# One late run of a causal convolution, moved from TensorE to VectorE and GpSimd

## The chip, the cores and the metric

The kernel runs on one core of one Trainium2 chip. The metric is the device time of one execution in microseconds (us), as the median of several runs; lower is better. A profile of one execution stands beside it, with the span from its first to its last instruction. The engines are called by the names of the profile: PE (TensorE, matmuls; PEld are its weight loads), DVE (VectorE), ACT (ScalarE), POOL (GpSimd) and SP (SyncE, which here only issues DMAs).

## The reference

Block-causal attention feeds a gated unit whose gate is a causal convolution in time. Inputs are q, k and v (8 batches, 8 heads, 576 positions, 64 features each), w_val and w_out (512 x 512) and conv_w (5 taps x 512 features):

```
mask   = block_i >= block_j                  # blocks of 64 positions
attn   = softmax(where(mask, q k^T / 8, -1e9))
x      = (attn v), heads side by side        # (8, 576, 512)
xp     = x with 4 zero rows in front of each batch
gate_pre[:, s, c] = sum over k < 5 of conv_w[k, c] * xp[:, s + k, c]
gate   = 1 / (1 + exp(-gate_pre))
out    = (gate * (x w_val)) w_out            # float32, (8, 576, 512)
```

The convolution is by feature: output feature c reads feature c alone, at five positions.

## The kernel before

**The order of the work.** A schedule written out in the string PLAN sets everything. Each word is one step, `name/arguments/engine/PSUM banks`, and the words are played in order: on each engine the instructions stand in the order of their words. "V/9.1/P/5" is step V for run 9 and quarter 1, on PE, into bank 5. The eight PSUM banks are handed out by hand, so a step that writes a bank waits for the step that read it last.

**Attention.** The work goes by p = 0 to 31, four pairs of heads for each of the eight batches (b = p // 4). `lq`, `lk`, `lv` load a block of 512 positions (v in two halves); `lt`, `lvt` load the last 64 positions of a batch. `cq`, `ct`, `cv`, `cvt` convert them to fp16 (mostly on POOL). `T`, `TT` transpose q and k on PE and `Te`, `TTe` copy them out of PSUM. `S` makes scores on PE, in three parts for each p, and `E` takes their exponential on ACT into the tile pt; `SL`, `EL` do so for the last block. `mka`, `mkb` write zeros over masked corners of pt (POOL). `A` and, once for a batch, `AT` multiply by v. `N`, `NT` divide by the sums (DVE). `X`, `XT` transpose the result and `Xe`, `XTe` copy it to xt, which holds features on partitions and positions along the free axis: four groups g of 128 features, and a ring of four batches of 4 + 576 columns, 2320 in all. Head pair p of batch b writes group g = p mod 4.

**The gated unit.** It does not follow batches but runs of RUN = 464 columns of the ring, five to a turn of the ring, n = 0 to 9. Run 7 covers ring columns 928 to 1392: the end of batch 5 and the first part of batch 6, so it needs `Xe` of p = 24 to 27. `C` computes the convolution of a run on PE: for each of five taps, 16 products with a diagonal 32 x 32 matrix of tap weights (tile DG, lines 585 to 595), 80 small matmuls into four banks. In doing so it moves the features: output partition 32 g + i of bank row x holds feature 128 g + 32 x + i, and `cwv` puts the columns of w_val in the same order, so that gate and value meet. `CS` takes tanh of half of it on ACT, two banks at a time, into the tile th (three buffers, run n in buffer n mod 3); `V` makes x w_val for a quarter of the features and a run; `Ve` computes (th + 1) times V into gv (DVE, line 614); the factor 0.5 is in w_out. `O u.t` multiplies 128 positions of gv by w_out (u is a pair of batches, t = 0 to 8; the last tile is split in two halves, `OL`), `Oe` copies the result to one of six osb tiles, `Od` stores it. Run 7 is read by O 2.7, O 2.8, O 3.0 and O 3.1.

**Weights of the taps.** `lcv` loads conv_w, `ccv` (line 362) makes it fp16, `CW` (line 551) turns it so that features lie on partitions, `CWe` copies it out and makes DG. `w0` are matmuls on zeros whose result nobody reads.

The shared helpers give one line to many steps in a profile: L137 are all matmuls, L141 all transposes on PE, L232 the copies by DVE and POOL, L230 those by ACT. L442 is E, L599 is CS, L614 is Ve.

The profiled program ends its PE order with: C 7, V 7.1, V 7.2, A 30, V 7.3, V 7.0, X 30, AT 7, C 8, V 8.0, XT 7, V 8.2, V 8.3, V 9.0, V 8.1, O 3.0, C 9, V 9.1, V 9.2, V 9.3, O 2.8, O 2.7, OL 1, OL 0, O 3.2, O 3.1, O 3.5, O 3.3, O 3.6, O 3.7, O 3.4.

Of the kernel before, what the change touches and what calls it, by code (L numbers as in the profile page):

```python
# [12 lines left out]
lk/0/S pdve//V ppool//G w0/1.128.0/P/3 lcv//S lq/0/S cq0/0/V ccv//G lk/1/S lq/1/A cq/1/V lt/0.0/S  # L13
lq/3/S lt/0.1/S lk/4/S lq/4/S ct/0/G lk/3/S CW//P/4 CWe//V lk/2/S lq/2/S cq/2/G lv/1.0/S lt/1.0/S
lv/0.0/S cq0/1/A pact//A T0/1/P/0+1 T0e/1/A lt/1.1/S T0/0/P/6+7 T0e/0/A S/0.1/P/5+6 T/1/P/0+1 Te/1/V
E/0.1/A lv/0.1/S lv/3.0/S lk/5/S lv/1.1/S lq/5/S S/0.0/P/5+6 E/0.0/A mka/0/G lt/2.0/S lt/2.1/S
lv/2.1/S lk/6/S TT/0/P/2+3 TTe/0/V SL/0/P/0+1 EL/0/A S/1.0/P/3+4 lv/3.1/S lq/6/S S/0.2/P/6+7
w0/1.64.1/P/5 E/1.0/A cq/4/V cq/3/V lvt/0/S E/0.2/A lv/2.0/S T/4/P/0+1 lq/8/S lk/8/S lq/7/S
S/1.1/P/2+3 E/1.1/A lk/7/S T/3/P/4+5 S/1.2/P/6+7 E/1.2/A Te/4/V S/4.0/P/0+1 lv/4.1/S T/2/P/2+3
E/4.0/A Te/3/V S/3.1/P/4+5 E/3.1/A mkb/0/G S/3.0/P/6+7 cv/0/G A/0/P/0+1 E/3.0/A S/4.1/P/4+5 Te/2/V  # L20
S/3.2/P/2+3 N/0/V mka/1/G cv/1/V ct/1/G cq/5/G TT/1/P/6+7 TTe/1/V w0/1.64.0/P/0 S/2.2/P/0+1 ct/2/G
E/4.1/A mkb/1/G mka/4/G E/3.2/A X/0/P/4+5 cv/3/G Xe/0/V E/2.2/A cq/6/G mkb/3/G mkb/2/G cvt/0/G
cv/2/G lv/7.0/S lv/5.0/S lv/4.0/S lwv/1/S S/2.1/P/2+3 E/2.1/A lwv/0/S lwo/0/S lwo/1/S T/5/P/4+5
Te/5/V lk/9/S lq/9/S lv/6.0/S lv/5.1/S cq/8/G lv/6.1/S lq/10/S lk/10/S mka/3/G cq/7/G lk/12/S
lq/12/S S/4.2/P/6+7 E/4.2/A mkb/4/G w0/1.64.0/P/0 S/2.0/P/0+1 E/2.0/A SL/1/P/2+3 EL/1/A A/1/P/4+5
N/1/V TT/2/P/6+7 TTe/2/V S/5.0/P/0+1 S/5.2/P/2+3 T/6/P/4+5 Te/6/V lq/13/S X/1/P/6+7 Xe/1/V E/5.0/A
lv/7.1/S lvt/1/S E/5.2/A mkb/5/G AT/0/P/0 NT/0/V lk/11/S lk/13/S lq/11/S S/6.1/P/4+5 S/6.0/P/6+7
SL/2/P/2+3 E/6.0/A EL/2/A T/8/P/0+1 Te/8/V A/3/P/6+7 N/3/V S/5.1/P/2+3 E/6.1/A T/7/P/0+1 Te/7/V
S/8.2/P/4+5 mka/2/G A/2/P/6+7 S/7.1/P/0+1 N/2/V E/5.1/A cwv/1/G cwv/0/G mka/5/G mka/6/G cwo/0/G
X/3/P/2+3 Xe/3/V E/8.2/A X/2/P/6+7 S/6.2/P/4+5 Xe/2/V E/7.1/A S/8.0/P/2+3 E/6.2/A cq/9/G mkb/8/G  # L30
E/8.0/A cv/5/G mkb/6/G cv/4/V C/0/P/0+1+6+7 A/4/P/4+5 XT/0/P/2 V/0.0/P/3 CS/0.1/A N/4/V X/4/P/4+5
CS/0.0/A Xe/4/A Ve/0.0/V S/7.0/P/0+1 E/7.0/A cwo/1/V XTe/0/V V/0.3/P/7 mka/7/G Ve/0.3/V V/0.2/P/3
Ve/0.2/V cv/6/G W//P/0+1+4+5 We/1/V S/7.2/P/6+7 V/0.1/P/2 We/0/A T/9/P/0+1 Te/9/V E/7.2/A
S/8.1/P/4+5 E/8.1/A A/5/P/6+7 S/9.0/P/0+1 A/6/P/4+5 Ve/0.1/V O/0.1/P/2 N/5/V E/9.0/A N/6/V X/5/P/0+1
Xe/5/A cq/10/G T/10/P/6+7 Te/10/V cq/12/G S/9.1/P/4+5 E/9.1/A O/0.2/P/3 Oe/0.2/V T/12/P/0+1 Te/12/V
S/10.0/P/6+7 mkb/7/G cv/7/G E/10.0/A cvt/1/G S/10.1/P/4+5 E/10.1/A O/0.0/P/3 X/6/P/6+7 Xe/6/A
Oe/0.0/A mka/8/G Oe/0.1/A lt/3.0/S lt/3.1/S A/7/P/0+1 AT/1/P/4 lv/8.0/S lt/4.0/S lt/4.1/S
S/12.0/P/6+7 mka/9/G lv/8.1/S N/7/V X/7/P/0+1 NT/1/V cq/11/G Xe/7/V lv/10.1/S E/12.0/A XT/1/P/5
XTe/1/V lv/10.0/S S/9.2/P/2+3 T/11/P/0+1 Te/11/V C/1/P/4+5+6+7 E/9.2/A cq/13/G T/13/P/2+3 V/1.1/P/0
CS/1.0/A lv/9.1/S Te/13/V lv/9.0/S lvt/2/S lv/11.1/S CS/1.1/A S/11.0/P/4+5 S/11.2/P/2+3 ct/3/G  # L40
TT/3/P/6+7 mkb/9/G TTe/3/V Ve/1.1/V cv/8/G V/1.3/P/1 Ve/1.3/V E/11.0/A lv/11.0/S lk/15/S
S/13.2/P/6+7 lq/15/S E/11.2/A S/10.2/P/4+5 mka/10/G lk/16/S V/1.0/P/0 Ve/1.0/V E/13.2/A A/8/P/2+3
N/8/V S/11.1/P/6+7 ct/4/G TT/4/P/0+1 TTe/4/V cv/10/G lq/16/S E/10.2/A lk/14/S lq/14/S V/1.2/P/5
Ve/1.2/V mkb/10/G mkb/11/G A/10/P/2+3 N/10/V mkb/13/G SL/3/P/0+1 E/11.1/A S/13.0/P/6+7 EL/3/A cv/9/G
E/13.0/A cvt/2/G A/9/P/4+5 X/8/P/0+1 Xe/8/A cv/11/G AT/2/P/2 S/12.1/P/6+7 E/12.1/A X/10/P/0+1 N/9/V
mka/11/G A/11/P/4+5 Xe/10/A O/0.3/P/3 NT/2/V XT/2/P/2 XTe/2/A lq/17/S SL/4/P/0+1 EL/4/A cq/15/G
T/15/P/6+7 N/11/V lk/17/S lv/13.1/S Oe/0.3/V S/13.1/P/4+5 Te/15/V O/0.4/P/2 S/12.2/P/0+1 lv/13.0/S
Od/0.0/S X/11/P/6+7 Oe/0.4/V lk/18/S lq/18/S E/13.1/A X/9/P/4+5 w0/1.64.1/P/3 w0/1.64.1/P/3
# [12 lines left out]
Xe/15/A Oe/0.8/V T/20/P/2+3 Te/20/A Xe/12/V lv/19.1/S lq/22/S lt/6.0/S lv/17.0/S X/14/P/4+5
S/19.1/P/0+1 E/19.1/A Xe/14/V X/13/P/6+7 A/16/P/4+5 lv/17.1/S lk/22/S Xe/13/V C/3/P/2+3+6+7 CS/3.0/A
N/16/V X/16/P/4+5 Xe/16/V lv/19.0/S lk/23/S Od/0.6/S O/0.7/P/0 cq/21/G lq/24/S Od/0.5/S T/21/P/2+3
Te/21/V lv/20.1/S lv/20.0/S CS/3.1/A lk/24/S Oe/0.7/V ct/6/G lq/23/S S/18.2/P/4+5 E/18.2/A mkb/18/G
cq/22/G V/3.2/P/1 Ve/3.2/V S/20.0/P/6+7 E/20.0/A C/4/P/2+3+4+5 CS/4.0/A V/3.3/P/0 Ve/3.3/V CS/4.1/A
V/3.1/P/7 Ve/3.1/V S/21.1/P/2+3 E/21.1/A mkb/17/G S/19.2/P/0+1 S/19.0/P/4+5 cv/18/G cvt/4/G cv/19/G
mka/17/G cv/17/G lt/7.1/S E/19.2/A mkb/19/G V/3.0/P/6 Ve/3.0/V V/4.3/P/3 lv/21.0/S lvt/5/S
TT/6/P/0+1 TTe/6/V E/19.0/A mka/19/G lq/25/S Od/0.7/S lv/21.1/S lk/25/S lt/7.0/S lk/26/S
S/20.2/P/6+7 E/20.2/A O/1.1/P/2 Ve/4.3/V S/20.1/P/0+1 E/20.1/A cq/24/G S/18.0/P/4+5 T/22/P/6+7
Te/22/V lq/26/S Oe/1.1/A O/1.2/P/3 A/17/P/0+1 E/18.0/A mka/18/G S/22.0/P/6+7 E/22.0/A AT/4/P/2  # L70
N/17/V X/17/P/4+5 S/21.0/P/0+1 E/21.0/A Xe/17/A A/19/P/6+7 Oe/1.2/V lv/23.1/S lv/23.0/S Od/1.1/S
lk/27/S O/1.3/P/3 NT/4/V lq/27/S XT/4/P/2 cq/23/G N/19/V lv/24.0/S lk/29/S S/21.2/P/0+1 T/24/P/6+7
# [40 lines left out]
def kernel(  # L113
# [44 lines left out]
    def one(b):  # L158
        return PS[0:128, b]
# [562 lines left out]
```

## Time and profile before

| | us |
|---|---|
| median of 3 runs | 187.36 |
| lowest, highest | 186.05, 188.68 |
| the profiled execution: its own time | 188.06 |
| its span, first to last instruction | 186.3 |
| PE, ACT, DVE, POOL busy | 164.2, 137.0, 125.1, 82.7 |
| last matmul ends, last copy out ends | 182.3, 182.9 |

The profiled execution's time is 1.76 us more than its span. A row of a timeline reads: start, duration, engine, line, operation, written tile <- read tiles, partitions x elements and type, xcount; in brackets the idle time of the engine before it and what ended it. Neighbouring instructions of one kind are merged into one row. A row by stretch reads: the stretch, its length, then busy time (and instructions) of PE, PEld, DVE, ACT and POOL, then the granted PE clock, the DMA share and GB/s. Of the chain by time, each row is a start, a length and what the chain went through.

### The profile page before, as it was taken

What the parts mean: (1) busy time and instruction counts of PE and PEld (TensorE: products, weight loads), DVE (VectorE), ACT (ScalarE), POOL (GpSimd) and SP (SyncE); (2) the same over time, 40 slices, a digit from 0 to 9 for tenths busy, and PEclk for the clock granted to TensorE, in tenths of its full rate; (3) what the DMA queues carried; (4) which work ended last, traced back from release to release, by engine and by line L of the source; (5) the groups of instructions that cost most, each with busy time, mean ns of one, the idle gap of its engine ahead of it and who ended that gap; (6) DMA issues with size and microseconds to landing.
All of it is one profiled execution on the core that took longest, in us unless ns stands there. A gap on an engine that the chain in (4) does not pass through costs nothing.

```text
span 186.3 us, 8262 instructions
## 1 busy us (share of the span) xinstructions
PE 164.2 (88%) x3534; PEld 101.4 (54%) x3534; DVE 125.1 (67%) x223; ACT 137.0 (74%) x164; POOL 82.7 (44%) x198
## 2 busy tenths in 40 slices
PE   1587638889999996999999999999999999999991
PEld 0364417754565774467645564656665575565540
DVE  5676636749977886777854677799787587533731
ACT  4489963698699885999969998897999842453431
POOL 6206449265682754556407455757590360000000
PEclk9999975699999999999999999999999999999999
DMA  6897896998966899769968888999998110351175
GB/s 184 261 286 180 223 262 172 291 328 243 267 165 157 224 308 300 191 165 327 273 157 272 239 245 260 298 286 282 222 276 231 69 60 0 141 204 57 69 281 217
DMA packets 66493, 40.38 MB, mean 217 GB/s; under 512 B 40213, under 2 KB 60949, under 8 KB 66458
## 3 DMA queue, kind: packets, MB, share of 16 engines
q1 hardware_dynamic: 66186, 39.61, 74.2%
q8 instruction: 27, 0.44, 1.0%
q10 hardware_dynamic: 272, 0.26, 0.4%
q14 instruction: 8, 0.07, 0.1%
HBM read 30.42 MB, written 9.44 MB: 214 GB/s over the span
## 4 chain that ended last, share of the span: by engine, by line
PE 74%; DMA 8%; DVE 5%; ACT 4%; SPq 4%; issue 3%; POOL 1%; DVEq 0%; ACTq 0%; POOLq 0%
PE PS L137 66%; PE PS L141 8%; DMA qks<-in_q_dram 3%; DMA qks<-in_k_dram 3%; ACT pt L442 3%; DMA vs<-in_v_dram 2%; DVE qkT L232 2%; SPq L244 2%; SPq L267 1%; DVE x L492 1%; ACT qkT L230 1%; POOL qk L232 1%; DVE rc L491 0%; DVE kt L232 0%; POOL v L232 0%
## 5 line engine op out<-in xcount | busy, mean ns | idle before, releaser
L442 ACT ACTIVATE pt<-PS 128x1024 f16<-128x1024 f32 x96 | 94.0, 1029 | 16.7 <-PE PS L137 15.1
L232 DVE COPY qkT<-PS 128x1024 f16<-128x1024 f16 x27 | 33.0, 1224 | 14.6 <-PE PS L141 13.7
L232 POOL CAST qk<-qks 128x1024 f16<-128x1024 f32 x28 | 29.1, 1042 | 25.3 <-DMA qks<-in_q_dram 14.8
L137 PE MATMUL PS<-qkT 64*128 64x384 f16 (+3 forms) x256 | 34.4, 319 | 2.9 <-ACT pt L442 1.6
L137 PE MATMUL PS<-xt,w_val 128*128 128x464 f16 x160 | 36.4, 360 | 0.0
L137 PE MATMUL PS<-w_out,gv 128*128 128x512 f16 (+2 forms) x164 | 35.5, 376 | 0.0
L137 PE MATMUL PS<-v,pt 128*128 128x65 f16 (+1 forms) x896 | 32.5, 198 | 2.4 <-POOL v L232 1.4
L137 PEld LDWEIGHTS <-pt 128*128 128x128 f16 (+1 forms) x960 | 29.5, 105 | 8.5 <-issue 4.5
L614 DVE SCALAR_TENSOR_TENSOR gv<-th,PS 128x464 f16<-128x464 f32 x40 | 24.6, 633 | 13.1 <-PE PS L137 7.8
L137 PEld LDWEIGHTS <-qkT 64*128 64x128 f16 x512 | 17.9, 97 | 16.6 <-issue 12.5
L599 ACT ACTIVATE th<-PS 128x928 f32<-128x928 f32 x20 | 17.9, 945 | 7.2 <-PE PS L137 7.0
L492 DVE TENSOR_TENSOR x<-PS,rc 128x512 f16<-128x512 f32 x32 | 22.1, 691 | 1.1
L232 POOL CAST v<-vs 128x512 f16<-128x512 f32 x30 | 18.5, 619 | 7.0 <-DMA vs<-in_v_dram 4.6
L137 PEld LDWEIGHTS <-w_val 128*128 128x128 f16 x160 | 13.5, 97 | 13.0 <-issue 2.4
L137 PEld LDWEIGHTS <-gv 128*128 128x128 f16 (+1 forms) x164 | 12.9, 100 | 12.9 <-issue 1.5
L141 PE MATMUL PS<-ident,qk 64*128 64x64 f16 x512 | 15.6, 202 | 3.3 <-POOL qk L232 3.0
L232 DVE COPY osb<-PS 128x512 f32<-128x512 f32 x20 | 13.7, 687 | 5.8 <-PE PS L137 5.8
L141 PEld LDWEIGHTS <-qk 64*128 64x128 f16 x512 | 12.4, 102 | 8.0 <-POOL qk L232 3.9
L464 POOL MEMSET pt<- 64x256 f16 x32 | 9.8, 306 | 13.3 <-ACT pt L442 12.2
L230 ACT COPY osb<-PS 128x512 f32<-128x512 f32 x15 | 8.7, 591 | 8.6 <-PE PS L137 8.4
L491 DVE RECIPROCAL rc<-PS 128x8 f32<-128x8 f32 x32 | 6.6, 206 | 12.2 <-PE PS L137 6.8
L137 PE MATMUL PS<-xt,DG 32*32 32x464 f16 x800 | 13.1, 358 | 0.4 <-ACT pt L442 0.3
(60 smaller groups left out, 136.4 us busy)
## 6 DMA issues: line engine op xcount, KB each, us to landing
out_dram<-osb SPq DMA_DIRECT2D x35, 256.0 KB, 3.9
qks<-in_k_dram SPq DMA_DIRECT2D x32, 256.0 KB, 4.8
vs<-in_v_dram SPq DMA_DIRECT2D x64, 128.0 KB, 4.4
qks<-in_q_dram SPq DMA_DIRECT2D x31, 256.0 KB, 5.2
tls<-in_q_dram SPq DMA_DIRECT2D x16, 64.0 KB, 3.5
tls<-in_k_dram SPq DMA_DIRECT2D x16, 64.0 KB, 3.6
vts<-in_v_dram SPq DMA_DIRECT2D x8, 128.0 KB, 5.2
gv<-in_moe_w_val_dram SPq DMA_DIRECT2D x2, 512.0 KB, 6.0
```

Source lines behind the costliest of these rows:

```text
L137: made.append(nc.tensor.matmul(out=out, lhsT=lhsT, rhs=rhs, start=start, stop=stop, skip_group_check=True))
L141: made.append(nc.tensor.transpose(out=out, in_=in_, identity=identity))
L230: i = nc.scalar.copy(out=out, in_=in_)
L232: i = (nc.vector if eng == "V" else nc.gpsimd).tensor_copy(out=out, in_=in_)
L244: DMA[eng].dma_start(out=rot(qks, p)[0:128, i], in_=(q, k)[i][b, 2 * g:2 * g + 2, 0:512, 0:64].rearrange("h (p n) d -> p h (n d)", n=4))
L267: DMA[eng].dma_start(out=tls[b % 2][0:128, i, r], in_=(q, k)[i][b, 0:8, 512:576, 0:64].rearrange("(g r) (p n) d -> r p g (n d)", r=2, n=2)[r])
L442: made.append(nc.scalar.activation(out=rot(pts, p)[0:128, 0:2, 512 * t:512 * t + 512], in_=both(take("S", p, t)), func=AF.Exp, bias=0.0, s ...
L464: nc.gpsimd.memset(pt[64:128, 0:2, 0:1024].rearrange("p h (t s) -> p h t s", t=2)[:, :, :, 0:64], 0.0)
L491: made.append(nc.vector.reciprocal(out=rc[0:128], in_=r[:, :, :, 64:65]))
L492: made.append(nc.vector.tensor_tensor(out=rot(x16, p)[0:128].rearrange("p i h d -> p h i d"), in0=r[:, :, :, 0:64], in1=rc[0:128].to_broad ...
L599: made.append(nc.scalar.activation(out=rot(ths, n)[0:128, 2 * i:2 * i + 2], in_=both(take("C", n, i))[:, :, 0:RUN], func=AF.Tanh, bias=0.0 ...
L614: made.append(nc.vector.scalar_tensor_tensor(out=gv[0:128, x, o:o + RUN], in0=rot(ths, n)[0:128, x], scalar=1.0, in1=one(take("V", n, x))[ ...
```

## The change

Run 7's convolution is no longer done on PE. The word C/7 is gone, and two kinds of steps come in:

- `lx 7.x` (x = 0 to 3): four DMAs from SBUF to SBUF on SP's queue, each 32 partitions x 468 columns, copy the features of run 7 from xt to a new tile xp, in the order of partitions in which C leaves them. Each needs all four groups of xt.
- `Q 7.x.k` (k = 0 to 4): one tap for the features of x, 128 x 464. Tap 0 is one multiplication by the tap's weight of each partition. On DVE (7 of the 20 steps) a later tap is one scalar_tensor_tensor, xp times weight plus th into th. On POOL (13 of the 20) it is two instructions: a multiplication into the tile part, and an addition of part to th. All five taps of an x add to the same part of th, so they follow each other across the two engines.

CS 7 then reads th from SBUF instead of PSUM, and writes it in place. ccv and CW make a second, permuted copy of the tap weights (tile taps, fp32), and the small tiles of the weights share their space with xp; part shares its space with olast, the tile of the last output.

The plan is a new one throughout: from its first word on the order of steps, the engines of some copies and the banks differ. Among them, by count: Te on ACT 8 instead of 4 (DVE 23 instead of 27), Oe on ACT 21 instead of 15 (DVE 14 instead of 20), TTe on ACT 1 instead of 0, w0 3 instead of 6, the first lq on SP instead of ACT, the last two stores on ACT instead of SP. Of the plan only the words of the tail are shown.

```diff
 PLAN = """
...
-N/30/V V/7.3/P/7 V/7.0/P/2 CS/7.1/A Ve/7.3/V Ve/7.2/V Od/1.6/S Oe/2.3/A Od/2.5/S X/30/P/0+1 Xe/30/A
-Od/2.3/S AT/7/P/3 C/8/P/0+1+5+6 CS/8.1/A V/8.0/P/7 NT/7/V XT/7/P/3 V/8.2/P/4 Ve/8.2/V V/8.3/P/6
-XTe/7/A V/9.0/P/3 V/8.1/P/4 Ve/8.3/V Ve/7.0/V O/3.0/P/2 Od/2.1/S CS/8.0/A Ve/8.0/V Od/2.2/S Oe/3.0/A
-C/9/P/0+1+6+7 CS/9.0/A V/9.1/P/5 V/9.2/P/2 V/9.3/P/0 Od/2.4/S Od/2.6/S Od/3.0/S Ve/9.0/V CS/9.1/A
...
+NT/6/V X/27/P/6+7 Xe/27/V V/6.0/P/5 XT/6/P/4 Xe/26/V XTe/6/A S/30.1/P/0+1 S/31.0/P/2+3 S/30.2/P/6+7
+V/6.2/P/4 Ve/6.0/V E/30.1/A A/28/P/0+1 N/28/V V/6.3/P/5 Ve/6.3/V mka/30/G mkb/31/G cv/29/G E/31.0/A
+mka/31/G A/29/P/2+3 N/29/V A/31/P/0+1 N/31/V Ve/6.2/V E/30.2/A mkb/30/G A/30/P/6+7 lx/7.3/S
+Q/7.3.0/G X/29/P/2+3 Xe/29/A lx/7.1/S AT/7/P/5 Q/7.1.0/G Od/1.7/S O/1.6/P/0 NT/7/V XT/7/P/1 Oe/1.6/A
+XTe/7/A O/2.6/P/4 Q/7.3.1/G lx/7.2/S lx/7.0/S Q/7.1.1/G Q/7.1.2/G X/28/P/2+3 N/30/V X/31/P/0+1
+Xe/31/V X/30/P/6+7 O/2.4/P/5 Od/2.2/S Q/7.1.3/G Xe/30/A Xe/28/V C/8/P/0+1+2+3 Od/1.8/S V/8.0/P/6
+V/8.1/P/7 Q/7.0.0/V Q/7.2.0/G Q/7.2.1/V Q/7.2.2/G Oe/2.4/A V/9.3/P/5 CS/8.1/A CS/8.0/A Ve/8.1/V
+C/9/P/0+1+2+3 Oe/2.6/A CS/9.1/A V/7.1/P/4 Q/7.2.3/G O/2.3/P/7 Od/1.6/S Q/7.0.1/G Q/7.3.2/V Q/7.3.3/G
+Q/7.1.4/V CS/9.0/A V/9.0/P/3 Oe/2.3/A Q/7.0.2/V V/7.0/P/2 V/9.2/P/7 V/7.2/P/0 Ve/9.3/V V/9.1/P/5
+V/7.3/P/1 Q/7.0.3/V Ve/9.0/V Q/7.2.4/G Q/7.0.4/V Q/7.3.4/G CS/7.1/A CS/7.0/A Ve/9.2/V V/8.3/P/7
+Ve/9.1/V OL/0/P/5 Ve/7.0/V OL/1/P/2 OLe/1/A V/8.2/P/3 Ve/7.3/V Ve/7.1/V Ve/7.2/V O/3.0/P/2 OLe/0/V
+Od/2.4/S Od/2.3/S Od/2.6/S Oe/3.0/A Od/3.0/S O/2.8/P/5 Oe/2.8/A Od/2.8/S Ve/8.2/V Ve/8.3/V OLd/0/A
+O/2.7/P/7 Oe/2.7/A Od/2.7/S O/2.5/P/3 Oe/2.5/A Od/2.5/S Ve/8.0/V O/3.1/P/5 Oe/3.1/A Od/3.1/S
...
+    stage = const([128, 2048], fp16, "stage")
+    conv_nat = stage[0:5, 0:1024].bitcast(fp32)
+    conv16 = stage[0:5, 1024:1536]
+    conv16x = stage[0:5, 1536:2048]
+    xp = stage[0:128, 0:4 * (RUN + 4)].rearrange("p (x s) -> p x s", x=4)
+    taps = const([128, 4, 5], fp32, "taps")
...
+    part = olast_all[0:128, 0:RUN]
...
     def ccv(eng, bank=None):
-        copy(eng, conv16[0:5, 0:512], conv_nat[0:5, 0:512])
+        copy(eng, conv16, conv_nat)
+        copy(eng, conv16x.rearrange("k (x j i) -> k x j i", x=4, j=4),
+             conv_nat.rearrange("k (j x i) -> k x j i", j=4, x=4))
...
+    @op
+    def lx(n, x, eng="S", bank=None):
+        o = RUN * (n % 5)
+        for g in range(4):
+            DMA[eng].dma_start(out=xp[32 * g:32 * g + 32, x],
+                               in_=xt[32 * x:32 * x + 32, g, o:o + RUN + 4])
+
+    @op
+    def Q(n, x, kk, eng, bank=None):
+        pooled.add(n)
+        t = rot(ths, n)[0:128, x]
+        xk, w = xp[0:128, x, kk:kk + RUN], taps[0:128, x, kk:kk + 1]
+        e = nc.vector if eng == "V" else nc.gpsimd
+        if kk == 0:
+            e.tensor_scalar(out=t, in0=xk, scalar1=w, scalar2=None, op0=ALU.mult)
+        elif eng == "V":
+            e.scalar_tensor_tensor(out=t, in0=xk, scalar=w, in1=t, op0=ALU.mult, op1=ALU.add)
+        else:
+            e.tensor_scalar(out=part, in0=xk, scalar1=w, scalar2=None, op0=ALU.mult)
+            e.tensor_tensor(out=t, in0=part, in1=t, op=ALU.add)
+
     @op
     def CS(n, i, eng, bank=None):
+        if n in pooled:
+            t = rot(ths, n)[0:128, 2 * i:2 * i + 2]
+            nc.scalar.activation(out=t, in_=t, func=AF.Tanh, bias=0.0, scale=0.5)
+            return
```

In the words, P is PE, V is DVE, A is ACT, G is POOL and S is SP.

## The prediction

> **What bounds the kernel now.** I read the page's first two parts, then its chain of waits with the chain by time, then the busy time by stretches, then the timeline of the last 30 us.
>
> ```profile
> span 186.3 us, 8262 instructions
> PE 164.2 (88%) x3534; PEld 101.4 (54%) x3534; DVE 125.1 (67%) x223; ACT 137.0 (74%) x164; POOL 82.7 (44%) x198
> PEclk9999975699999999999999999999999999999999
> PE 74%; DMA 8%; DVE 5%; ACT 4%; SPq 4%; issue 3%; POOL 1%; DVEq 0%; ACTq 0%; POOLq 0%
> ```
> ```profile
> 20.74 5.73 DMA qks<-in_q_dram
> ...
> 162.91 2.85 PE PS L137 x123
> 165.76 0.11 PE PS L141 x2
> 165.87 16.44 PE PS L137 x160
> 182.31 0.02 issue
> 182.33 0.59 ACT osb L230
> ```
> ```profile
> 15.40:25.60 10.20, 6.21 (x148) 4.28 (x144) 6.17 (x10) 9.86 (x12) 4.54 (x10) 1.00 0.83 215
> 25.60:35.90 10.30, 7.67 (x164) 6.46 (x164) 5.48 (x8) 4.24 (x5) 5.76 (x13) 0.50 0.81 231
> 35.90:46.00 10.10, 8.63 (x210) 4.82 (x207) 6.86 (x14) 8.75 (x10) 6.17 (x12) 1.00 0.98 295
> ```
> ```profile
> 157.57 1.27 PE L137 MATMUL PS<-xt,DG 32*32 32x464 f16 x80
> 158.78 1.74 PE L137 MATMUL PS<-xt,w_val 128*128 128x464 f16 x8
> ...
> 171.00 2.52 PE L137 MATMUL PS<-xt,w_val 128*128 128x464 f16 x12
> 173.36 8.93 PE L137 MATMUL PS<-w_out,gv 128*128 128x512 f16 x48
> ```
> TensorE is the bound: 74% of the chain is PE, and from 146 us on nothing else is in it but the last eviction. Two stretches differ. Up to 38 us PE is idle for 15 us: it waits for transfers, the longest time (2.77 us before 27.68) for the q block issued at 20.74 and landed 5.73 us later; and from 25.6 to 35.9 us the granted clock is 0.50. From 41 us to 182.3 us PE runs almost without a gap. A whole convolution of a run (C 7, the 80 small matmuls at 157.57) holds PE for only 1.2 us, since many run at once. ScalarE, VectorE and GpSimd are far from full at the end: GpSimd does nothing at all after 156.2 us. A saving must come from PE; a wait put in front of PE in the last 30 us costs its full length.
>
> **Removed.** C 7's 80 matmuls: 158.78 - 157.57 = 1.2 us of PE in a stretch without gaps: -1.2. Its four PSUM banks come free too, worth nothing there, as PE waits for no bank in the tail.
>
> **Added, small.** Four more 5-column matmuls in CW (the four of now took 0.26), a 20-column copy in CWe (0.17), a second small copy of the weights (GpSimd took 0.60 for one; now both are VectorE's). All lie in the first 8 us, where PE waits for the first q and k; they are part of the start's sum.
>
> **Moved: the start.** The whole order is written anew, so even work that the change does not touch moves. Before C 0 both orders do the same: 24 exponentials, T 0 to 8, A 0 to 3, X 0 to 3. Now C 0 begins at 38.10. In the new order q 6 is asked for after 2 v halves and 5 tail pairs instead of 7 and 6, so SP reaches it at about 15 us (14 q/k blocks at 0.5 each, 5 pairs at 1.2) instead of 20.74; by the 0.8 us that a q/k block takes to land behind another it lands near 19, not 26.5. The 2.77 us stall goes; then ScalarE is late next: its 24 exponentials at 0.91 (start to start), three short ones at 0.6, the 0.7 us copy of tails that it now has, and two features at 0.6, from the first at about 8.9 us, end at 8.9 + 21.8 + 1.8 + 0.7 + 1.2 = 34.4, with 1 us of waits for T 4 and tail 1: C 0 near 35.4 at best, a gain of 2.7. Against it: the window of half clock can come again (PE's duty stays near 6 in 10 us) and the spare w0 matmuls that keep PE busy are three instead of four. Ends: -3 and +1; I take -1.5, half of the stall. Between C 0 and C 6 PE's work is the same; ScalarE's rises by about 3 us of 84 (four Te at 1.02 move to it), beside PE's 100: nothing.
>
> **Moved: the tail.** I count t from the end of X 27, the last transposed features that run 7 needs (148.55 now). PE steps, start to start: V 0.78, O 0.86, A 0.62, AT 0.76, C 1.2, OL 0.43, S 0.22, X 0.12. Added up in the new order: C 8 at 9.6, V 9.3 at 12.4, C 9 at 13.2, O 2.3 at 15.2, V 9.1 at 19.1, OL 1 at 21.9, O 3.0 at 23.1, then 11 output steps to the end at 32.8. O 3.0, 2.8, 2.7 read run 7's gate, and OL 1 takes the bank of Ve 7.0: all of Q must be done by then.
> Transfers: Xe 26 ends at t = 1.2 (NT 6 0.6, two copies 0.42). Four lx of four DMAs behind it on SP, 0.4 us an issue, landing 2.0 us after issue (the olast row, the nearest small one; a 256 KB row has 3.9 in traffic, but there is little here: 60 GB/s): x = 3 at 4.4, x = 1 at 6.0, x = 2 at 8.0, x = 0 at 9.6. Behind them on SP are only output transfers, with osb buffers to spare. GpSimd is free at 4.5 (mkb 30 behind E 30.2).
> GpSimd's prices: one input, 464 columns: casts of 512 and 1024 columns took 0.619 and 1.042, so 0.58. An add of two fp32 inputs does not occur. Low end 0.58 (as one input), high end 1.16 (two passes); it reads 928 elements, nearest to the 1024-column cast, so 0.95. With 0.06 between instructions (as in the timeline) a tap costs GpSimd 1.64. VectorE's tap is a scalar_tensor_tensor, 0.63 like gv.
> The chain: Q 7.3.0 ends 5.1, 7.1.0 6.6, then four taps to 13.2, 7.2.0 to 13.9. VectorE must wait for that with Q 7.2.1 (it stands idle from about 10.5, and Ve 8.1 behind it, so O 2.3 loses a little): 14.6. Then GpSimd's last six taps, 7.2.2, 7.2.3, 7.0.1, 7.3.3, 7.2.4, 7.3.4, at 1.64 end at 24.4. VectorE waits for 7.0.1 (19.5) with Q 7.0.2; Ve 9.3 is behind it, so V 9.1 starts at 20.8. CS 7.1 and 7.0 (0.945 and 0.9) end at 26.3, Ve 7.0 at 27.0 (OL 1 waits for it), Ve 7.3, 7.1, 7.2 at 28.8. O 3.0 starts at 28.8 instead of 23.1: +5.7. The cover that the edit counts on is the 17 us from C 8 to O 3.0; the chain is longer.
> Low end: an add at 0.58 ends the chain at 20.8, O 3.0 at 25.1: +2.0. High end: an add at 1.16 (+2.1), and each of four VectorE taps holding GpSimd up for its 0.63 (+2.5): +10.3.
>
> *A rule beside it.* No row shows VectorE and GpSimd both at two-input work. The Trainium skill (SBUF — State Buffer, "SBUF: two separate sides") says that a VectorE instruction with two SBUF inputs and a GpSimd instruction exclude each other for their whole length; by it rival 2 below, 193.6, would be the likeliest.
> The Trainium skill (GPSIMD Engine Reference, 3.1) gives 4497 ns for an fp32 add of 2048 columns, an estimate of 1.02 us for 464: the sum would then be 0.7 higher.
>
> **Sum.** The profiled execution took 188.06 (span 186.3 and 1.76 around it); the median of the runs is 187.36, their spread 2.6, so I leave the 0.7 in. 188.06 - 1.2 - 1.5 + 5.7 = 191.1.
>
> **Rivals.** (1) The chain is covered, not slower: GpSimd's add costs 0.58 and the start gains its 3: 188.06 - 1.2 - 3 + 2.0 = 185.9; with the start at -1.5, 187.4. For it: GpSimd's memsets and casts are cheap; against: none reads two tensors. It decides where the add is under about 0.65.
> (2) The two engines hold each other up: + 2.5, 193.6. For it, an alternating dependence; against, no row.
> (3) The clock falls in the tail. In 15.4 to 25.6 us PE was busy for 6.21 of 10.2 us, and the next 10.3 were granted at 0.50; at 7.67 it came back. In my tail PE works some 5 of the 10 us from t = 19 to 29. If the same happens, the ten output steps after it (8.6 us) take up to twice as long: taken at two thirds, +6: 197. It depends on where the windows fall.
> (4) The start goes the wrong way, by new waits at the same prices: +1 instead of -1.5: 193.6.
>
> **How the numbers follow.** Forecast (chain late by 4 to 7.5, 189 to 193): 0.42. Rival 1 (185.5 to 189): 0.22. Rivals 2 and 4 (193 to 195.5): 0.16. Rival 3 (195.5 to 200): 0.16. Gain beyond rival 1, below 185: 0.04. The range 186 to 197 leaves out about 2 in 10. About 2% is what these runs can tell from no change: below 183.6 with 0.03; above 191.1 about half of the forecast (0.20) and rivals 2, 3 and 4 (0.32): 0.52; between: 0.45. Forecast alone: 189 to 193.
>
> **What would show it.** In the profile after: GpSimd's tensor_tensor near 0.95 (0.58 and 1.16 are the rivals' ends), its last one 20 us after its first; PE gaps before V 9.1, OL 1 and O 3.0, released by VectorE, of 5 to 6 us in all; C 0 near 36.6; SCALAR_TENSOR_TENSOR on th longer than 0.63 if the engines exclude each other; PEclk under 9 in the last slices for rival 3. I am wrong if PE goes from V 9.1 to O 3.0 with less than 3 us of gaps, or if C 0 comes after 38.

## The result, and the profile after

| | before | after |
|---|---|---|
| median, us | 187.83 (4 runs, 186.05 to 188.68) | 208.88 (4 runs, 205.88 to 209.24) |
| the profiled execution, its span | 188.06, 186.3 | 208.82, 207.0 |
| X 27 ends | 148.55 | 148.43 |
| O 3.0 starts | 168.84 | 192.31 |

The change makes the kernel slower: ratio 1.108, 95% interval 1.093 to 1.124. The forecast was 191.1 with a range of 186 to 197; the time lies 11.9 us above the range. Ratios, here and below, compare only the runs of each kernel that lie within 1.5% of its fastest, so they can differ a little from the quotient of the medians.

The page of the profile after, the same parts as were shown of before:

```profile
span 207.0 us, 8180 instructions
PE 168.2 (81%) x3455; PEld 100.6 (49%) x3455; DVE 125.5 (61%) x224; ACT 142.8 (69%) x173; POOL 113.1 (55%) x220
PEclk9999999999999999969999999999999966985699
PE 56%; POOL 14%; DVE 11%; ACT 6%; issue 5%; DMA 5%; SPq 1%; POOLq 1%; DVEq 0%; ACTq 0%
```

PE has 79 instructions less and is busy longer, mainly because some of them ran at half clock (the four matmuls of O 2.3 below took 1.86 us, those of O 1.6 at full clock 1.04). GpSimd was 1% of the chain that sets the end and is 14% now. Where it sits shows in the chain by time (start, length, what):

```profile
155.77 1.45 POOL th L627
157.22 1.43 POOL olast L631
158.65 0.07 issue
158.72 1.18 POOL th L632
...
184.68 1.44 POOL olast L631
...
186.16 1.21 POOLq L758
...
187.40 1.85 ACT th L638 x2
...
189.27 0.65 DVE gv L655
...
189.96 13.41 PE PS L138 x56
```

From 155.77 to 187.38 the end hangs on GpSimd alone. L627 and L631 are its multiplications, L632 its additions (the last addition is the piece marked POOLq). Between them there are only gaps of issue: no VectorE tap and no transfer is the last to be waited for. Behind them come the tanhs of run 7 on ACT (L638), its first gate product on VectorE (L655), and PE. The groups of the steps on run 7's gate (count | busy, mean ns | idle before, what ended it):

```profile
L631 POOL TENSOR_SCALAR olast<-stage,taps 128x464 f32<-128x464 f16 x10 | 15.5, 1551 | 0.8
L627 POOL TENSOR_SCALAR th<-stage,taps 128x464 f32<-128x464 f16 x3 | 4.3, 1446 | 1.4 <-DVE gv L655 1.3
L629 DVE SCALAR_TENSOR_TENSOR th<-stage,taps,th 128x464 f32<-128x464 f16 x6 | 6.5, 1094 | 11.2 <-POOL th L627 6.8 <-POOL th L632 4.4
L638 ACT ACTIVATE th<-th 128x928 f32<-128x928 f32 x2 | 1.8, 968 | 13.5 <-POOL th L632 13.5
```

GpSimd hardly idles (0.8 and 1.4 us in all); VectorE and ScalarE wait for it 11.2 and 13.5 us. And PE's timeline of the tail, with its waits in brackets:

```profile
171.44 1.86 PE L138 MATMUL PS<-w_out,gv 128*128 128x512 f16 x4 [6.78 <-DVE gv L655]
173.09 3.93 PE L138 MATMUL PS<-xt,w_val 128*128 128x464 f16 x16
179.57 1.73 PE L138 MATMUL PS<-xt,w_val 128*128 128x464 f16 x8 [2.54 <-DVE gv L655]
182.62 0.94 PE L138 MATMUL PS<-xt,w_val 128*128 128x464 f16 x4 [1.33 <-DVE gv L655]
183.40 0.60 PE L138 MATMUL PS<-w_out,gv 128*128 128x256 f16 x4
189.96 1.01 PE L138 MATMUL PS<-w_out,gv 128*128 128x256 f16 x4 [5.96 <-DVE gv L655]
190.77 1.75 PE L138 MATMUL PS<-xt,w_val 128*128 128x464 f16 x4
192.31 11.04 PE L138 MATMUL PS<-w_out,gv 128*128 128x512 f16 x48
```

Four waits, 16.6 us in all, before O 2.3, V 9.1, V 8.3 and OL 1, each ended by a gate product of VectorE (`gv L655`). The first two of these products stood in VectorE's queue behind a tap that waited for GpSimd, the third behind a tap that was slow beside GpSimd (1.43 us), and the fourth, run 7's own, behind the tanhs that waited for GpSimd's last addition. By stretches of 3.41 us (PE, PEld, DVE, ACT, POOL busy, then the granted clock):

```profile
85.59:89.00 3.41, 1.51 (x45) 0.99 (x40) 0.56 (x2) 2.05 (x3) 1.85 (x4) 1.00 1.13 312
89.00:92.42 3.42, 3.42 (x44) 1.86 (x43) 2.72 (x6) 1.94 (x2) 0.20 (x1) 0.50 0.88 254
164.10:167.51 3.41, 0.55 (x3) 0.20 (x2) 0.00 (x0) 1.54 (x2) 3.15 (x4) 1.00 0.02 5
167.51:170.92 3.41, 0.00 (x0) 0.00 (x0) 1.17 (x2) 0.00 (x0) 3.41 (x3) 0.50 0.00 0
170.92:174.34 3.42, 2.90 (x8) 1.07 (x8) 2.97 (x3) 0.59 (x1) 3.15 (x4) 0.50 0.00 0
...
177.75:181.17 3.42, 1.60 (x8) 0.78 (x8) 2.90 (x5) 0.00 (x0) 3.24 (x3) 1.00 0.00 0
181.17:184.58 3.41, 1.50 (x9) 0.78 (x8) 1.95 (x3) 0.00 (x0) 3.23 (x3) 1.00 0.00 0
184.58:187.99 3.41, 0.00 (x0) 0.00 (x0) 0.00 (x0) 0.59 (x1) 2.60 (x2) 0.50 0.00 0
187.99:191.41 3.42, 1.45 (x6) 0.84 (x6) 2.14 (x4) 1.62 (x3) 0.00 (x0) 0.50 0.00 0
191.41:194.82 3.41, 3.41 (x9) 1.18 (x8) 2.21 (x5) 0.51 (x1) 0.00 (x0) 0.50 0.02 5
```

The clock changes only where these stretches meet. In these rows it falls to 0.50 after one in which PE was busy for 1.51 us or less, and comes back after one of 2.90 or more. PE's busy time alone does not decide it, though: in the trace of the kernel before the clock fell after a stretch with 2.06 us busy (22.21 to 25.63), and in that of e4 below it fell after one with 1.87 (86.33 to 89.75) and stayed after one with 1.73 (178.49 to 181.90). What the rule is stays open; the long waits, at any rate, have half clock after them. That of 167.51 to 174.34 shows no price, as PE has to wait again before V 9.1; that of 184.58 to 194.82 lies on the path from OL 1 on.

Two theories were to be told apart, with a third behind them. A: GpSimd's own instructions are the length of the chain. B: VectorE and GpSimd hold each other up. C: the new order of the whole plan, or the clock, makes the loss.

### The profile page after: what moved, and what is told of

Read it like the earlier page. It is cut to its first block, busy times and chain, and to the rows that moved or that the text cites. A ratio compares the mean times of both kernels' runs of the same rounds, so it can differ in the third digit from the quotient of the medians.

```text
span 207.0 us, 8180 instructions
## 1 busy us (share of the span) xinstructions
PE 168.2 (81%) x3455; PEld 100.6 (49%) x3455; DVE 125.5 (61%) x224; ACT 142.8 (69%) x173; POOL 113.1 (55%) x220
## 4 chain that ended last, share of the span: by engine, by line
PE 56%; POOL 14%; DVE 11%; ACT 6%; issue 5%; DMA 5%; SPq 1%; POOLq 1%; DVEq 0%; ACTq 0%
PE PS L138 50%; POOL olast L631 8%; PE PS L142 6%; POOL th L632 5%; DVE qkT L240 4%; ACT pt L452 4%; DMA qks<-in_k_dram 3%; DVE x L502 3%; DMA qks<-in_q_dram 2%; POOL th L627 1%; DVE gv L655 1%; ACT qkT L238 1%; ACT th L638 1%; DVE rc L501 1%; POOLq L758 1%
## 5 line engine op out<-in xcount | busy, mean ns | idle before, releaser
L452 ACT ACTIVATE pt<-PS 128x1024 f16<-128x1024 f32 x96 | 93.5, 1034 | 12.3 <-PE PS L138 10.4
L138 PE MATMUL PS<-w_out,gv 128*128 128x512 f16 (+2 forms) x164 | 39.2, 400 | 12.7 <-DVE gv L655 12.7
L138 PE MATMUL PS<-xt,w_val 128*128 128x464 f16 x160 | 38.0, 371 | 4.5 <-DVE gv L655 3.9
L138 PE MATMUL PS<-qkT 64*128 64x512 f16 (+3 forms) x256 | 33.9, 324 | 4.9 <-ACT pt L452 1.0
L655 DVE SCALAR_TENSOR_TENSOR gv<-th,PS 128x464 f16<-128x464 f32 x40 | 24.6, 632 | 15.8 <-PE PS L138 8.0
L240 DVE COPY qkT<-PS 128x1024 f16<-128x1024 f16 (+1 forms) x24 | 28.7, 1199 | 6.4 <-PE PS L142 6.2
L138 PE MATMUL PS<-v,pt 128*128 128x65 f16 (+1 forms) x896 | 31.1, 195 | 0.5 <-POOL tl L240 0.3
L138 PEld LDWEIGHTS <-qkT 64*128 64x128 f16 x512 | 18.5, 100 | 16.4 <-issue 10.0
L238 ACT COPY osb<-PS 128x512 f32<-128x512 f32 x21 | 12.4, 590 | 16.6 <-PE PS L138 15.4
L640 ACT ACTIVATE th<-PS 128x928 f32<-128x928 f32 x18 | 16.3, 954 | 7.2 <-PE PS L138 7.2
L480 POOL MEMSET pt<- 64x128 f16 x32 | 6.7, 213 | 20.6 <-ACT pt L452 15.0
L240 DVE COPY xt<-PS 128x512 f16<-128x512 f16 (+1 forms) x28 | 10.8, 405 | 9.1 <-PE PS L142 9.0
L631 POOL TENSOR_SCALAR olast<-stage,taps 128x464 f32<-128x464 f16 x10 | 15.5, 1551 | 0.8
```

The source lines that it names most:

```text
L138: made.append(nc.tensor.matmul(out=out, lhsT=lhsT, rhs=rhs, start=start, stop=stop, skip_group_check=True))
L238: i = nc.scalar.copy(out=out, in_=in_)
L240: i = (nc.vector if eng == "V" else nc.gpsimd).tensor_copy(out=out, in_=in_)
L452: made.append(nc.scalar.activation(out=rot(pts, p)[0:128, 0:2, 512 * t:512 * t + 512], in_=both(take("S", p, t)), func=AF.Exp, bias=0.0, s ...
L480: nc.gpsimd.memset(rot(pts, p)[64:128, 0:2, 1024:1088], 0.0)
L631: e.tensor_scalar(out=part, in0=xk, scalar1=w, scalar2=None, op0=ALU.mult)
```

## The experiments

### Run 7 back on TensorE, in the new order (C)

The first try, e1_pe_conv, takes lx and Q out and puts C 7 back in:

```diff
-... lx/7.3/S Q/7.3.0/G ... Xe/28/V C/8/P/0+1+2+3 ... Q/7.3.4/G CS/7.1/A CS/7.0/A ...
+... Xe/28/V Oe/2.4/A C/7/P/0+1+2+3 CS/7.1/A CS/7.0/A V/8.0/P/6 V/8.1/P/7 V/9.3/P/5 C/8/P/0+1+2+3 ...
```

> The changed kernel's new order, but run 7's convolution is back on PE (C 7 before C 8, lx and Q left out, CS 7 from PSUM). Theory A (the whole loss is the chain of taps in the tail, above all GpSimd's instructions at 1.45 and 1.16 us): X 27 still ends near 148.4, then 32.8 us of PE steps, 1.2 of C 7 and some 0.5 of waits for banks: last matmul near 183, time 186 to 190, as before. Rival C (the new order, or the clock in it, is what costs): well above that, 195 or more.

It took 193.98 us (189.96 to 195.11), between the two expectations. Two of PE's waits, 1.65 us before O 2.3 and 1.09 before V 9.0, came from the order I had spliced in, which also lets the copy of O 2.3 into its buffer before O 1.6 has been sent from there, so that those 128 rows of the output hold others. It decides nothing, so I wrote that tail anew, in e1b_pe_conv: V 7.0 to 7.2 between C 7 and C 8, V 7.3 and runs 8 and 9 after them, and each transfer ahead of the copy that takes its buffer.

> The order of the changed kernel up to X 28, with run 7 convolved by TensorE again (C 7 stands where X 28 has been copied out) and the words behind it put in an order with no waits for banks; no permuted copy and no taps. If the taps' chain makes the loss (theory A), the order itself is about neutral: in the changed kernel 37.3 us of TensorE work are left at X 27, 1.2 us more with C 7, and 185.5 us was the same sum before; so 187 to 191. If the new order or its clock makes the loss (theory C): 195 or more.

189.89 us, ratio 1.016 (1.011 to 1.021). PE waits for 1.06 us in the whole tail and the clock is full. So the new order up to X 28, with run 7 on PE and a tail of its own, costs 2 to 4 us, and the other 19 or so of the 21 us belong to the moved convolution and the tail written round it: C accounts for little.

### All taps on VectorE (A against B)

```diff
-Q/7.0.0/V Q/7.2.0/G Q/7.2.1/V Q/7.2.2/G ...
+Q/7.3.0/V Q/7.3.1/V Q/7.3.2/V Q/7.3.3/V Q/7.3.4/V ...     (x = 3, 1, 2, 0; none on G)
```

> All 20 taps on VectorE, none on GpSimd (order of VectorE's own steps in the tail rearranged round them). Theory A: a VectorE tap takes 0.69 as where it ran alone, 20 of them some 13 us, in a row from 10 us after X 27, with the Ve steps between; O 3.0 some 28 us after X 27 instead of 43.9: time 193 (190 to 196). Rival C: above 200.

196.06 us, ratio 1.046 (1.041 to 1.052): 12.8 us come back by taking GpSimd out. VectorE's groups in it:

```profile
L629 DVE SCALAR_TENSOR_TENSOR th<-stage,taps,th 128x464 f32<-128x464 f16 x16 | 11.2, 701 | 0.6
L627 DVE TENSOR_SCALAR th<-stage,taps 128x464 f32<-128x464 f16 x4 | 1.8, 454 | 0.0
```

All twenty taps take VectorE 13.0 us; thirteen of them took GpSimd 31.5. Alone, a VectorE tap is 0.70 us, not the 1.09 that it was on average beside GpSimd. The time is 3 us above theory A's number, just past its range: O 3.0 starts 30.4 us after X 27, not 28. PE still waits 4.17 us before OL 1, now for VectorE, and the clock is at 0.50 from 175.77 to 182.59. Without GpSimd nothing can hold VectorE up either, so this run does not yet part A from B.

### Is it the weight that GpSimd reads for each partition?

```diff
+        if eng == "G":
+            w = 0.25
```

> GpSimd multiplies by the constant 0.25 instead of each partition's own weight, so that the output is not the reference's; nothing else differs. If the weight read for each partition is what makes GpSimd's multiplication take 1.45 us: near 0.58 each, 13 of them, 11 us less: 197 to 198. If the multiplication from fp16 to fp32 costs that by itself: 1.45 again and 209.

207.59 us, ratio 1.108 (1.103 to 1.114). GpSimd's multiplications that nothing disturbs are 1.37 us instead of 1.45. It is the multiplication, not the read of a weight.

### Two links less

Tap 4 of two of the four parts is left out (Q 7.2.4 and Q 7.3.4, the last two on GpSimd).

> The last two taps of GpSimd (7.2.4 and 7.3.4) are left out, so that the output is not the reference's. Theory A: the chain stands on the path link by link, so two taps of 2.7 to 2.9 us come off in full: 203 to 204. Rival B (waits between the two engines make the length): less than half of it, 206 to 209. Rival C: nothing.

199.6 us (196.88 to 200.59), ratio 1.056 (1.047 to 1.065): some 9 us less for two links. The two profiled executions, 208.82 and 200.53, lie 8.3 us apart, and this splits in two. OL 1 starts 6.0 us earlier, at 183.95, the length of two taps (1.71 + 1.16 + 1.44 + 1.16 + gaps). The other 2.3 us are the clock: PE's wait before OL 1 falls from 5.96 to 0.12 us, and with it the second half-clock stretch, so that the work from OL 1 to the end of PE's work takes 11.1 us instead of 13.41. My number left this second effect out.

### The prices by themselves

Behind the last output of the kernel before, blocks of equal instructions on 464 columns, first GpSimd alone, then VectorE alone, then side by side; the total time of this kernel means nothing.

```diff
+    times(3, G.tensor_copy, out=a, in_=h)
+    times(3, G.tensor_scalar, out=a, in0=h, scalar1=0.25, scalar2=None, op0=mul)
+    times(3, G.tensor_scalar, out=a, in0=h, scalar1=w, scalar2=None, op0=mul)
...
+    times(6, G.tensor_tensor, out=a, in0=b, in1=g, op=add)
+    taps_v(8)
```

> The kernel before, and behind its last output a row of instructions on spare tiles, 128 x 464, whose results nobody reads: GpSimd alone (copy fp16 to fp32; multiplication by a constant; by each partition's weight, from fp16, from fp32, to fp16; addition of two fp32 tiles), VectorE alone (multiplication; scalar_tensor_tensor with two SBUF inputs), then VectorE's scalar_tensor_tensor beside GpSimd's addition, multiplication, copy and memset. Theory A: alone, copy 0.58, constant 0.58 to 0.7, weight 1.45, addition 1.16; VectorE 0.69 alone. Rival B (the engines exclude each other for whole instructions): VectorE's 0.69 becomes 1.7 to 1.9 beside GpSimd's additions, and little changes beside memsets. If they do not: 0.69 throughout.

GpSimd's rows (start, duration of the block, count at the end): alone, then beside VectorE's taps:

```profile
181.15 1.84 POOL L709 CAST qks<-pt 128x464 f32<-128x464 f16 x3
183.09 4.28 POOL L709 TENSOR_SCALAR qks<-pt 128x464 f32<-128x464 f16 x3
187.47 4.52 POOL L709 TENSOR_SCALAR qks<-pt,rc 128x464 f32<-128x464 f16 x3
192.08 4.51 POOL L709 TENSOR_SCALAR qks<-qks,rc 128x464 f32<-128x464 f32 x3
196.57 4.52 POOL L709 TENSOR_SCALAR pt<-pt,rc 128x464 f16<-128x464 f16 x3
201.06 3.63 POOL L709 TENSOR_TENSOR qks<-qks,qks 128x464 f32<-128x464 f32 x3
...
211.24 9.20 POOL L709 TENSOR_TENSOR qks<-qks,qks 128x464 f32<-128x464 f32 x6
...
221.96 10.19 POOL L709 TENSOR_SCALAR qks<-pt,rc 128x464 f32<-128x464 f16 x6
```

VectorE's taps: six alone, then eight beside the additions, the multiplications, ten copies in fp32 and sixteen memsets of GpSimd:

```profile
206.59 4.39 DVE L709 SCALAR_TENSOR_TENSOR qks<-pt,rc,qks 128x464 f32<-128x464 f16 x6
...
211.15 10.53 DVE L709 SCALAR_TENSOR_TENSOR qks<-pt,rc,qks 128x464 f32<-128x464 f16 x8
...
221.85 6.93 DVE L709 SCALAR_TENSOR_TENSOR qks<-pt,rc,qks 128x464 f32<-128x464 f16 x8
...
232.57 7.17 DVE L709 SCALAR_TENSOR_TENSOR qks<-pt,rc,qks 128x464 f32<-128x464 f16 x8
...
241.85 5.85 DVE L709 SCALAR_TENSOR_TENSOR qks<-pt,rc,qks 128x464 f32<-128x464 f16 x8
```

A cast of 464 columns is 1.84 / 3 = 0.61 us, as the forecast had it; a multiplication of the same columns is 1.43 (constant) or 1.51 with the gap between two, two and a half times a cast. An addition is 1.21 with its gap. Side by side, start to start: VectorE's tap goes from 0.73 to 1.52 beside additions (six of the eight; the first and the last met none) and to 0.87 in the mean beside multiplications, and stays 0.73 beside memsets; an addition goes to 1.53, a multiplication to 1.70 in the mean of six. So B exists, as a surcharge of 0.1 to 0.8 us an instruction; a tap beside additions stays below the 1.7 to 1.9 us that exclusion for whole instructions would have meant.

### Multiplications on ScalarE, additions left on GpSimd (A against B, without changing the order)

```diff
+            nc.scalar.activation(out=m, in_=xk, func=AF.Copy, bias=0.0, scale=w)
+            if kk:
+                nc.gpsimd.tensor_tensor(out=t, in0=m, in1=t, op=ALU.add)
```

for the steps of GpSimd; `m` goes round four buffers, and the plan is that of the changed kernel, word for word.

> The changed kernel with GpSimd's 13 multiplications given to ScalarE (a copy with the weight as scale, four buffers in turn); GpSimd keeps only its adds, in the same order. Theory A (the 1.45 us multiplications are links of the chain): about 13 x 1.45 = 19 us go from GpSimd, its adds take 10 x 1.2 = 12 us beside VectorE's taps, O 3.0 comes by 180 instead of 192, 196 (192 to 200). Theory B (the engines' exclusion and the adds make the chain): the adds beside VectorE's taps cost as before, 203 or more.

190.37 us, ratio 1.018 (1.012 to 1.024). 18.5 us are gone by moving thirteen multiplications, more than theory A's own number and range. Between the profiled executions (208.82 and 191.04) it is 17.8: 1.5 because X 27 happens to end earlier (146.96), 15.2 between X 27 and the start of O 3.0 (175.66), and 1.1 behind it, with the clock full throughout. The groups:

```profile
L637 POOL TENSOR_TENSOR th<-qks,th 128x464 f32<-128x464 f32 x10 | 12.3, 1250 | 8.1 <-ACT qks L635 6.9 <-DVE th L629 1.0
L635 ACT ACTIVATE qks<-stage,taps 128x464 f32<-128x464 f16 x10 | 6.1, 677 | 0.0
L629 DVE SCALAR_TENSOR_TENSOR th<-stage,taps,th 128x464 f32<-128x464 f16 x6 | 6.0, 1018 | 3.1 <-POOL th L637 3.1
```

ScalarE multiplies in 0.61 us (6.1 / 10), about what the forecast had charged GpSimd for it. GpSimd now idles 8.1 us between its additions; VectorE's taps are as slow beside them as before (1.02 us). The slowing of B is still there (an addition takes 1.25 us in the mean), and the loss is not: A holds, and B is a small term.

### The clock after the waits

Spare matmuls on zeros fill the two long waits:

```diff
-... Q/7.2.3/G O/2.3/P/7 ... Ve/7.0/V OL/1/P/2 ...
+... Q/7.2.3/G w0/26.128.0/P/3 O/2.3/P/7 ... Ve/7.0/V w0/22.128.0/P/3 OL/1/P/2 ...
```

> The changed kernel with spare matmuls on zeros put where PE waits in the tail: 26 before O 2.3 and 22 before OL 1, each row shorter than the wait it fills. If the half clock after the gaps costs: the granted clock stays at 1.00 to the end, O 2.3 takes 1.03 instead of 1.86 and V 8.2, O 3.0 and O 2.8 about 1.0 instead of 1.4 to 1.9: 2.5 to 3.5 us less than the changed kernel, 205 to 206.5. If the clock has no part: the same 209.

204.85 us (204.02 to 207.43), ratio 1.097 (1.089 to 1.106). The span is 3.7 us shorter; 0.9 of it come from X 27, which in this execution ended at 147.53, and most of the rest from the end: the 56 matmuls from OL 1 on took 11.1 us instead of 13.4. The ratio's interval overlaps that of the changed kernel, so it is the trace, not the ratio, that shows the gain. The clock did not stay at 1.00 as expected: with the first wait filled, that before V 9.1 was longer (4.01 us instead of 2.54), and from 176.26 to 183.08 the clock was 0.50.

### Could the idea beat the kernel before?

All of run 7's dependents can stand last: runs 8 and 9 and the outputs other than O 2.7, O 2.8, O 3.0 and O 3.1 do not need its gate. Two kernels with that order, both with each part's first tap multiplied by ScalarE and the other sixteen taps on VectorE: e9 behind the new order, e10 behind the order of the kernel before.

```diff
+Q/7.3.0/A Q/7.3.1/V Q/7.3.2/V Q/7.3.3/V Q/7.3.4/V Ve/8.0/V ... C/9/P/0+1+2+3 ...
+... OL/1/P/6 ... OL/0/P/7 ... V/7.2/P/0 V/7.3/P/1 V/7.0/P/2 V/7.1/P/3 ... O/2.8/P/4 O/2.7/P/5 O/3.0/P/6 O/3.1/P/7
```

> The changed kernel's order up to X 28; then no tap on GpSimd: ScalarE multiplies the first tap of each part, VectorE adds the other 16 by its multiply-and-add, and TensorE does everything that does not need run 7 (runs 8 and 9, 11 other outputs) before V 7.0 to V 7.3 and O 2.8, 2.7, 3.0, 3.1. Theory A: VectorE has 16 x 0.73 = 12 us of taps and some 13 us of other work in the 25 us from the landing of the copy to V 7.0, so TensorE's waits in the tail shrink to under 2 us: 187 to 191, the 1.2 us of C 7 just about what is gained. If a copy by transfers and taps on VectorE cost more than C 7 wherever TensorE's order puts them: 194 or more.

> The same tail (taps by ScalarE and VectorE, run 7's products last) behind the order of the kernel before, up to its A 26, with X 26 moved up: whether the idea beats the kernel before at all. TensorE has 1.27 us less to do (C 7). If the taps are covered: 185.5 to 187.5 beside 187.8. If VectorE, which copies, normalises and gates in the same stretch, comes late by 2 us or more: 188 to 191.

Both missed: 197.23 us (ratio 1.050, 1.042 to 1.058) and 212.85 us (1.134, 1.127 to 1.141). In the first, VectorE idled 7.5 us before three of the four parts (2.87, 1.53, 3.08), because I had queued ScalarE's first taps behind tanhs and copies of other outputs. The second shows another price, in its chain by time:

```profile
152.65 0.41 SPq L618
153.11 0.58 SPq L618
...
160.70 0.59 SPq L618
161.34 2.26 DMA out_dram<-osb
163.62 0.59 ACT osb L239
164.26 2.96 PE PS L139 x24
```

Fourteen of the sixteen transfers of lx stand here one behind another, from 152.65 to 161.3, and hold SP 0.59 us each. I had put them ahead of the store of O 1.0, whose buffer the copy of O 1.6 needs, whose bank O 2.6 needs: PE stood for 12.15 us. In the changed kernel SP spends 12.6 us on the same transfers, their waits for the last features included.

With both mended (stores ahead of or between the transfers; two parts by ScalarE's multiplications and GpSimd's additions, two by VectorE):

> The order of the kernel before up to its A 26, with what the runs so far taught: multiplications of two of run 7's four parts by ScalarE (0.62 us each) with GpSimd's adds (1.2 us each), the other two parts by VectorE alone; the transfers of O 1.0, 1.8 and 1.6 put ahead of or between the 16 copies, whose issue holds SP for some 14 us and held TensorE for 12 us in the run before; run 7's products last. Theory: with the links cheap and SP's queue mended, nothing waits, and C 7's 1.27 us are all that can be gained: 185.5 to 187.5 beside 187.0. If a wait of over 1.5 us is left in the tail: 188 to 192.

> The changed kernel's order up to X 28 with the same division of the taps and run 7's products last, without ScalarE's late first taps that made VectorE wait 7.5 us in the earlier run of this order. Theory: at most the C 7 of the same order with TensorE's convolution (189.9) is gained: 187.5 to 190. If the division still leaves VectorE or ScalarE late by over 1.5 us: 191 or more.

The first takes 187.54 us (12 runs, 185.21 to 189.2), ratio 1.001 (0.996 to 1.006); the second 189.96, ratio 1.012 (1.005 to 1.019). PE waits 1.8 and 1.1 us in their tails. At its best the moved convolution gives nothing that can be measured: beside the 1.2 us of C 7 stand small waits of about that size, and no version here beats the kernel before.

## Why the prediction was wrong

The forecast said slower with 0.52 and by the right mechanism, a chain of taps that ends later than PE needs it; the size was wrong. By its own count from X 27, O 3.0 would start at 23.1 without waits, was forecast for 28.8 and started at 192.31 - 148.43 = 43.9: +15.1. X 27 itself: 148.43 against 147.05, +1.4. From O 3.0 to PE's end: 11.04 against 9.7, +1.3. Sum 17.8, the whole miss.

- **The step that failed**: "GpSimd's prices: one input, 464 columns: casts of 512 and 1024 columns took 0.619 and 1.042, so 0.58." A cast of 464 columns is indeed 0.61; the multiplication is 1.45. The 13 of them took 15.5 + 4.3 = 19.8 us where 13 x 0.58 = 7.5 had been summed: 12.3 of the 15.1, of which 1.0 belongs to rival 2 below. I took "one input" as what sets the price and gave no upper end to it, while the addition had two ends; so the range never held the truth. An operation that no row showed was priced as if a row showed it.
- **The addition**: 1.16 in the changed kernel, 0.95 taken, inside the ends of 0.58 and 1.16, at the top: 10 x 0.21 = 2.1 us. The Trainium skill (GPSIMD Engine Reference, 3.1), by which I had estimated 1.02, was the nearer.
- **The engines holding each other up (rival 2)**: real, but it is no rival to the size. On the path it shows as three multiplications of 1.71, 1.95 and 1.71 instead of 1.45, 1.0 us in all; VectorE's longer taps are not in the chain. The Trainium skill (SBUF — State Buffer, "Who interferes with whom") has an instruction with two SBUF inputs contend with a GpSimd instruction that reads SBUF, and not with one that only writes it: the memset rows agree. Exclusion over the whole length, which I had taken from that page ("SBUF: two separate sides"), is not what two-input work shows: an addition (1.21) and a tap (0.73) side by side came at one pair in 1.53, between the longer and the sum, 1.94.
- **The clock (rival 3)**: it came as well, not instead. Its price on the path was 2.3 us (13.4 - 11.1 from OL 1 on), not 6. The Trainium skill (TensorE: Matmul & The Clock Gate, "Part 1: The HAM clock gate") has a free-running window of 3413 ns and half clock after an idle one: the length agrees, but here a window with PE busy for 1.50 of 3.41 us was enough, and in the kernel before one with 2.06.
- **The transfers**: SP needs 5.40 / 2 = 2.7 us for each lx, not 4 x 0.4. The first part landed not before 151.1 (the landing of its fourth transfer is not in the trace), the others at 155.6, 160.2 and 161.4, that is 2.7 or more, 7.2, 11.8 and 13.0 after X 27, against 4.4, 6.0, 8.0 and 9.6. GpSimd idled at most 1.3 us by it (before 155.77), as it was late anyway.
- **The start**: right, and worthless. C 0 began at 35.29, the forecast's best end (35.4), 2.8 us earlier than before and behind the same work. But X 27 did not move. By stretches, PE's busy time is equal again by 148 us (129.5 and 129.9): it lost 1.8 us between 80 and 100 us, where it paused 1.90 us at 86.4 inside X 12, with 3.4 us of half clock after. The pages name nothing that PE waits for there. The traces do show something beside it: on the queue of instructions (q8, 27 transfers of 16 KB) one started at 85.92, and in each of the ten executions of the new order a pause of 0.6 to 2.3 us begins within 1.9 us behind the start of that transfer, the twelfth. Most other transfers of that queue have no such pause behind them, so that this is a likely cause, not a shown one. X 27 differs from execution to execution: in the ten of the new order it ended between 146.40 and 149.70, 148.1 in the mean; in four of the old one between 146.84 and 148.77, 148.0 in the mean. That "between C 0 and C 6 PE's work is the same" was true, and 1.5 us of gain should not have followed from it.
- **Two readings beside the sum**: "the 17 us from C 8 to O 3.0" are 13.5 by the forecast's own count (23.1 - 9.6), and in the old order X 26, not X 27, is the last that run 7 needs. Neither changes the sum.
- **What the experiments confirm, and what not**: with multiplications at 0.61 us, on ScalarE, O 3.0 starts 28.7 us after X 27 and the changed plan takes 190.37; the forecast, which priced them at 0.58 on GpSimd, had 28.8 and 191.1. So the multiplications on GpSimd were the loss. That the numbers agree this closely is luck: on ScalarE the multiplications run beside the additions instead of between them, and the additions, the transfers and the start all came out otherwise than the forecast had them.

## What to carry to other kernels

Price an instruction by a row of its own operation on its own engine; a cast is no row for a multiplication, even with the same tensor read and written. Where no such row exists, bound it upward as well, and multiply the bound by the number of links before trusting the sum: thirteen times 0.9 us was two thirds of the miss. Work handed to an idle engine is free only if its chain ends before its reader: here moving 1.2 us from the busiest engine bought a chain of 31.6 us, and even the best division of it tried here broke even.

## What the runs showed of the hardware

- GpSimd multiplies 464 columns in 1.37 us (constant) to 1.45 us (weight of each partition), the same from fp16 or fp32 and to fp16 or fp32 (4.51 and 4.52 us for three); it casts them in 0.61 and adds two fp32 tensors in 1.16 (1.21 from start to start). VectorE multiplies them in 0.45, ScalarE in 0.61.
- A VectorE multiplication that met a GpSimd addition took 1.44 us instead of 0.45, in the changed kernel and again (1.37) with the multiplications on ScalarE: nearly one addition longer. This form seems to wait for the addition to end, where the multiply-and-add shares; no run tries it by itself.
- A DMA from SBUF to SBUF of 32 partitions x 468 columns holds SP's queue for 0.59 us; fourteen in a row kept whatever stood behind them waiting for 8.7 us.
